# Soft-capped attention with an MLP: half-tile scores issued ahead of VectorE's reads of the same PSUM tile, and two tanh in the other order

## The chip, the cores and the metric

The kernel runs on one core of a Trainium2 chip. The metric is the device time of one execution in microseconds (us); for the kernel before it is the median of three runs. The profile is of one further execution.

## The reference

```python
scale = 1.0 / np.sqrt(q.shape[-1])                      # q, k, v: 4 x 12 x 448 x 64
scores = scale * np.matmul(q, k.transpose(0, 1, 3, 2))
scores = cap * np.tanh(scores / cap)                    # cap = 30
scores = scores - np.max(scores, axis=-1, keepdims=True)
attn = np.exp(scores)
attn = attn / (np.sum(attn, axis=-1, keepdims=True) + 1e-09)
x = np.matmul(attn, v)                                  # heads side by side: 1792 x 768
h = np.maximum(x @ w_in, 0.0)                           # w_in 768 x 2048
out = h * h @ w_out                                     # w_out 2048 x 768
```

Inputs are float32, the weights float64, which the kernel splits on the chip into two float32r words (`hi` and `lo`) each. A product of two split operands is three matmuls: hi by hi, hi by lo, lo by hi.

## The kernel before

Attention goes over 24 pairs of heads (`NP`), one pair in each turn of a loop over `n`; the two heads of a pair share the 128 partitions, 64 rows each. The 448 keys of a pair are handled in seven blocks of 64. Scores come transposed (keys in the partitions, queries along the row) in four tiles: tiles 1, 2 and 3 hold one block of keys of both heads, a "half" tile 0 the last block of both.

The score tiles lie in PSUM, in the pool `ps_s` of two buffers, each of shape 128 x 2 x 512: two halves of one PSUM bank each. In a turn they are handed out in the order tile 1, tile 2, `half`, tile 3, so that tile 1 and `half` use one buffer and tile 2 and tile 3 the other. Of the buffer of the half tile, `half[:, 0]` takes the half tile's own scores, and `half[:, 1]` takes the transposes of the next pair's q (line 347). The next pair's k is transposed into a tile of its own (`ps_t`, line 341). `take` reads the two transposed operands back on VectorE, two instructions each: a rounded copy `kqh` (line 356) and the rest `kql` (line 357); these are the operands of the next pair's scores (line 366).

ScalarE takes tanh of each score tile out of PSUM (line 373, scale 1/cap) and then exp in SBUF (line 378, scale cap). One turn behind, `sums` (line 386) adds up the probabilities with matrices of ones and `pv` (line 396) multiplies them by v. VectorE brings both to SBUF (lines 406 and 401); the sums go through DRAM (lines 408 to 425: gathered, inverted, broadcast to a tile `rb`), and `normalise` multiplies and splits the result (lines 430 to 434) a further two turns behind.

Beside that, VectorE and ScalarE decode weights of the first MLP layer in small steps (`decode`), and from n = 9 on a turn holds one `part`: six matmuls of the first layer (line 292) for a batch whose attention is done. After the loop come the rest of the first layer and the second layer (lines 661 to 663).

The attention loop runs under a manual schedule: on every engine the instructions stand in the order in which the Python code issues them. Waits between engines are put in by the framework, from the order in which the code issues accesses of the same tile. Loads of q go through SyncE's queue, those of k and v through GpSimd's.

Of the kernel before, what the change touches and what calls it, by code (L numbers as in the profile page):

```python
# [169 lines left out]
def tile_softcap_attention_mlp(ctx, tc, q, k, v, cap, w_in, w_out, out):  # L170
# [143 lines left out]
    def load_k(n, queues=(nc.sync, nc.sync)):  # L314
        for _ in load_keys(kn[n % NKQ], k, n, queues):
            pass

    def load_q(n, upper=(nc.sync, nc.sync), lower=None):
        b, j = divmod(n, NPAIR)
        for i in range(2):  # L320
            x = q[b, 2 * j + i].rearrange("(p t) d -> p t d", t=NS)
            upper[i].dma_start(out=qn[n % NKQ][top, 0:4, i], in_=x[:, 0:4])
            (lower or upper)[i].dma_start(out=qn[n % NKQ][bottom, 0:3, i], in_=x[:, 4:7])

    def load_v(n):
        for _ in load_keys(vn[n % NKV].rearrange("p h t d -> p t h d"), v, n, (nc.gpsimd, nc.gpsimd)):
            pass
# [9 lines left out]
    def transpose_k(n):  # L337
        tps[n, 0] = ps_t.tile([P, 512], F32, tag="t", name="tp")
        kf = kn[n % NKQ].rearrange("p t h d -> p t (h d)")
        for t in range(4):  # L340
            nc.tensor.transpose(tps[n, 0][:, t * P:(t + 1) * P], kf[:, t], ident)  # L341

    def transpose_q(n, tp):
        tps[n, 1] = tp
        qf = qn[n % NKQ].rearrange("p t h d -> p t (h d)")
        for t in range(3):
            nc.tensor.transpose(tp[:, t * P:(t + 1) * P], qf[:, t], ident)  # L347
        nc.tensor.transpose(tp[:, 3 * P:S], qf[top, 3], ident[top, top])

    def take(n, i, cast=nc.vector.tensor_copy):  # L350
        cols = (slice(0, 4 * P), slice(4 * P, 4 * P + S))[i]
        if i == 0:
            kqs[n] = [qp.tile([P, 4 * P + S], F32R, tag=x, name=x) for x in LATE]
        hi, lo = kqs[n]
        tp = tps.pop((n, i))[:, :cols.stop - cols.start]
        cast(out=hi[:, cols], in_=tp)  # L356
        nc.vector.tensor_sub(out=lo[:, cols], in0=tp, in1=hi[:, cols].bitcast(F32))  # L357

    def scores(n, u, sc=None):
        hi, lo = kqs[n]  # L360
        if sc is None:
            sc = ps_s.tile([P, 2, 512], F32, tag="s", name="sc")
        rows, t = ((top, bottom), u - 1) if u else ((slice(0, P),), 3)
        for s, (kx, qx) in enumerate(((hi, hi), (hi, lo), (lo, hi))):
            for h, r in enumerate(rows):
                nc.tensor.matmul(out=sc[:, h, :S], lhsT=kx[r, t * P:(t + 1) * P], rhs=qx[r, 4 * P:],  # L366
                                 start=(s == 0), stop=(s == 2))
        probs[n, u] = sc

    def tanh(n, u):  # L370
        c = 2 if u else 1
        p = pp.tile([P, c, S], F32, tag=f"p{c}", name="p", bufs=NPT if u else 2)
        nc.scalar.activation(out=p, in_=probs[n, u][:, :c, :S], func=ACTF.Tanh, scale=qks)  # L373
        probs[n, u] = p

    def exp(n, u):
        p = probs[n, u]
        nc.scalar.activation(out=p, in_=p, func=ACTF.Exp, scale=cap_sb)  # L378


    def sums(n):
        pvs[n, 1] = ps_v.tile([P, S], F32, tag="pb", name="pb")
        for u in (1, 2, 3, 0):
            for h in range(2):
                r = 32 * (h if u % 2 else 2 + h)
                nc.tensor.matmul(out=pvs[n, 1][r:r + 32], lhsT=ones if u else hones[:, h],  # L386
                                 rhs=probs[n, u][:, h if u else 0], start=(u in (1, 2)), stop=(u in (3, 0)),
                                 tile_position=(0, r))


    def pv(n):
        pvs[n, 0] = ps_v.tile([P, S], F32, tag="pa", name="pa")
        for u in range(NU):
            p, t = probs.pop((n, u)), (u - 1 if u else 3)
            for h, r in enumerate((top, bottom)):
                nc.tensor.matmul(out=pvs[n, 0][r], lhsT=vn[n % NKV][:, h, t], rhs=p[:, h if u else 0],  # L396
                                 start=(u == 0), stop=(u == NU - 1))

    def evac(n):
        es[n] = ep.tile([P, S], F32, tag="e", name="e", bufs=NE)  # L400
        nc.vector.tensor_copy(out=es[n], in_=pvs.pop((n, 0)))


    def take_sums(n):
        e = ep.tile([P, S], F32, tag="es", name="es", bufs=NE)
        nc.vector.tensor_copy(out=e, in_=pvs.pop((n, 1)))
        rds[n] = ep.tile([P - 16, 2, 8], F32, tag="cmp", name="cmp", bufs=NE)
        nc.sync.dma_start(out=rds[n][:, 0], in_=e[0:64:32])
        nc.sync.dma_start(out=rds[n][:, 1], in_=e[64:P:32])

    def invert(n):
        cmp = rds[n]
        nc.vector.scalar_tensor_tensor(out=cmp[:, 0], in0=cmp[:, 0], scalar=guard[:P - 16], in1=cmp[:, 1],
                                       op0=ALU.add, op1=ALU.add)
        nc.vector.reciprocal(out=cmp[:, 0], in_=cmp[:, 0])
        rd = dram.tile([2, S], F32, tag="rd", name="rd")
        nc.sync.dma_start(out=rd.rearrange("i (o c) -> (i o) c", c=8), in_=cmp[:, 0])
        rds[n] = rd


    def spread(n):
        rd = rds[n]
        rds[n] = ep.tile([P, S], F32, tag="rb", name="rb", bufs=2)
        for h, r in enumerate((top, bottom)):
            last["dma"] = nc.sync.dma_start(out=rds[n][r], in_=rd[h:h + 1].partition_broadcast(D))

    def normalise(n):
        b, j = divmod(n, NPAIR)
        x = ep.tile([P, S], F32, tag="x", name="x", bufs=1)
        nc.vector.tensor_mul(out=x, in0=es.pop(n), in1=rds.pop(n))  # L430
        xs = xpool.tile([P, 2, S], F32R, tag="xs", name="xs")
        hi, lo = xs[:, 0], xs[:, 1]
        nc.vector.tensor_copy(out=hi, in_=x)
        last["dve"] = nc.vector.tensor_sub(out=lo, in0=x, in1=hi.bitcast(F32))
        xh[b, j], xl[b, j] = hi, lo
# [24 lines left out]
    def prepare_cap():  # L460

        nc.vector.tensor_scalar_mul(ncap, cap_sb, -1.0)
        nc.vector.tensor_tensor(out=ncap, in0=ncap, in1=cap_sb, op=ALU.min)
        nc.vector.tensor_scalar(out=far, in0=ncap[0:1], scalar1=-CAP_MAX, scalar2=None, op0=ALU.is_lt)

        nc.scalar.activation(out=guard, in_=ncap, func=ACTF.Exp)
        nc.vector.tensor_scalar_mul(guard, guard, 1e-9)
# [24 lines left out]
    def part(pool=ps_m, tag="m"):  # L492
        b, f, o = parts.pop(0)
        if o == 0:
            hps[b, f] = pool.tile([P, 512], F32, tag=tag, name="hps")[:, :S]
        mlp1_part(b, f, o, 6)
        if o == 3 * KDM - 6:
            ends.append((b, f))

    def decode(count):  # L500
        for _ in range(count):
            next(decoding, None)


    for n in range(NP + 1):
        on, prep, old = n < NP, n + 1 < NP, n > 0
        more = n + 2 < NP

        if on:
            scores(n, 1)  # L510
            scores(n, 2)
            tanh(n, 1)
            tanh(n, 2)
            exp(n, 1)
            exp(n, 2)
        if more:
            load_q(n + 2)
            load_k(n + 2, (nc.gpsimd, nc.gpsimd))
            load_v(n + 2)
        if n == 0:  # L520
            prepare_cap()
        decode(1)

        if on:
            half = ps_s.tile([P, 2, 512], F32, tag="s", name="sc")
        if prep:
            transpose_k(n + 1)
            transpose_q(n + 1, half[:, 1])
            take(n + 1, 0)
            take(n + 1, 1)  # L530
        if on:
            scores(n, 0, half)
        if on and parts[0][1] in decoded and n >= NPAIR * (parts[0][0] + 1) + 3:
            part()
        if on:
            tanh(n, 0)
        if n >= 2:
            invert(n - 2)

        if on:  # L540
            scores(n, 3)
            tanh(n, 3)
            exp(n, 0)
            exp(n, 3)

        if n >= 3:
            normalise(n - 3)
        if old:
            sums(n - 1)
            take_sums(n - 1)  # L550
            pv(n - 1)
        if n >= 2:
            spread(n - 2)
        for b, f in ends:
            mlp1_end(b, f)
        ends.clear()
        decode(2 if n < 9 else 3)
        if old:
            evac(n - 1)
# [167 lines left out]
```

## Time and profile before

| | |
|---|---|
| time, median of three runs | 781.48 us (780.1 to 785.14) |
| profiled execution, time | 784.2 us |
| its span, first to last instruction | 782.4 us |
| TensorE busy | 721.2 us, 92% of the span |
| VectorE, ScalarE, GpSimd busy | 49%, 39%, 15% |
| mean granted TensorE clock | 0.954 of full speed |
| the attention loop | up to about 324 us |

The profile names engines PE (TensorE; PEld is its loading of weights), DVE (VectorE), ACT (ScalarE), POOL (GpSimd) and SPq (SyncE's DMA queue). L366 is line 366 of the kernel. A matmul's end is modelled, and a busy engine is not one at its peak. "A <- B" at a wait says that A stood idle until B was done.

### The profile page before, as it was taken

To read this page: it belongs to the slowest core of one execution; us is meant where nothing else is said; L and a number is where in the kernel's file an instruction comes from. 1 tells how busy PE (TensorE), PEld (TensorE's weight loads), DVE (VectorE), ACT (ScalarE), POOL (GpSimd) and SP (SyncE) were. 2 spreads that over 40 slices of the span, in tenths; PEclk is the share of its full clock that TensorE was granted. 3 is DMA by queue.
4 is the path that set the end of the run, shared out by engine and by line. 5 is a ranking of instruction groups with operands and counts; after the bars stand their busy time and mean duration, and the time that the engine had idled before them with its cause. 6 is when DMAs were issued, how large, how long until landed. Compare 5 with 4: busy or idle time off the path is not lost.

```text
span 782.4 us, 10711 instructions
## 1 busy us (share of the span) xinstructions
PE 721.2 (92%) x3978; PEld 575.5 (74%) x3978; DVE 383.3 (49%) x807; ACT 301.3 (39%) x430; POOL 114.1 (15%) x201
## 2 busy tenths in 40 slices
PE   6787787888878788999999999999999999999996
PEld 5333334445444454699899999999999999999995
DVE  3345555454554533455598999961896112111100
ACT  4657555554555554331353443421433212111100
POOL 8424424232242410010000000000000000000000
PEclk8799999898999889999999999999999999999998
DMA  7233424253243311151466456453563422342001
GB/s 169 57 80 89 109 56 104 59 112 84 67 110 81 92 51 25 49 178 65 137 217 187 134 192 192 152 168 113 172 206 95 125 75 75 93 124 79 22 21 34
DMA packets 95932, 83.11 MB, mean 106 GB/s; under 512 B 39072, under 2 KB 86688, under 8 KB 95872
## 3 DMA queue, kind: packets, MB, share of 16 engines
q1 hardware_dynamic: 86768, 68.50, 30.5%
q0 software_dynamic: 6112, 10.91, 5.9%
q10 hardware_dynamic: 2992, 2.93, 1.2%
q8 instruction: 33, 0.54, 0.3%
q14 instruction: 27, 0.22, 0.1%
HBM read 61.87 MB, written 20.27 MB: 105 GB/s over the span
## 4 chain that ended last, share of the span: by engine, by line
PE 90%; DVE 8%; ACT 1%; issue 0%
PE hps L292 31%; PE sc L366 11%; PE po L661 10%; PE po L662 10%; PE po L663 10%; PE pa L396 10%; PE pb L386 6%; DVE kql L357 4%; DVE kqh L356 4%; PE tp L341 2%; PE warm L443 1%; ACT p L373 0%; ACT p L378 0%; ACT osb L668 0%; PE tp L347 0%
## 5 line engine op out<-in xcount | busy, mean ns | idle before, releaser
L292 PE MATMUL hps<-xs,kqh 128*128 128x448 f32 x576 | 163.6, 365 | 1.3 <-DVE r L297 1.3
L661 PE MATMUL po<-ohi,gh 128*128 128x384 f32 x448 | 149.7, 335 | 0.6 <-ACT osb L668 0.6
L662 PE MATMUL po<-olo,gh 128*128 128x384 f32 x448 | 150.0, 335 | 0.0
L663 PE MATMUL po<-ohi,gl 128*128 128x384 f32 x448 | 148.4, 335 | 0.0
L373 ACT ACTIVATE p<-sc,qks 128x896 f32<-128x896 f32 (+1 forms) x96 | 85.0, 912 | 132.8 <-PE sc L366 131.5
L292 PEld LDWEIGHTS hps<-xs,kqh 128*128 128x128 f32 x576 | 108.1, 188 | 10.2 <-DVE r L297 1.7
L292 PE MATMUL hps<-xs,kql 128*128 128x448 f32 x288 | 105.2, 365 | 0.0
L366 PE MATMUL sc<-kqh 64*128 64x448 f32 (+1 forms) x168 | 47.6, 484 | 50.1 <-DVE kql L357 49.0
L614 DVE TENSOR_TENSOR gl<-graw,gh 128x2048 fp32r<-128x2048 f32 x14 | 32.1, 2291 | 124.3 <-ACT gh L613 114.0
L378 ACT ACTIVATE p<-p,cap_sb 128x896 f32<-128x896 f32 (+1 forms) x96 | 85.4, 941 | 0.0
L661 PEld LDWEIGHTS po<-ohi,gh 128*128 128x128 f32 x448 | 84.0, 188 | 0.9 <-ACT osb L668 0.9
L662 PEld LDWEIGHTS po<-olo,gh 128*128 128x128 f32 x448 | 84.1, 188 | 0.0
L663 PEld LDWEIGHTS po<-ohi,gl 128*128 128x128 f32 x448 | 84.0, 188 | 0.0
L366 PEld LDWEIGHTS sc<-kqh 64*128 64x128 f32 (+1 forms) x168 | 19.8, 202 | 80.4 <-DVE kql L357 52.2
L396 PE MATMUL pa<-p,vn 128*64 128x448 f32 x384 | 77.7, 547 | 0.0
L296 ACT ACTIVATE r<-hps 128x448 f32<-128x448 f32 x64 | 34.6, 541 | 84.0 <-PE hps L292 82.4
L396 PEld LDWEIGHTS pa<-p,vn 128*64 128x64 f32 x384 | 25.6, 138 | 54.0 <-issue 53.2
L292 PE MATMUL hps<-xs,whi 128*128 128x448 f32 x192 | 63.2, 415 | 0.0
L297 DVE TENSOR_TENSOR r<-hps,r 128x448 f32<-128x448 f32 x64 | 39.6, 620 | 48.0 <-ACT r L296 47.9
L613 ACT CAST gh<-graw 128x2048 fp32r<-128x2048 f32 x14 | 26.7, 1910 | 92.1 <-PE po L662 82.2
L292 PEld LDWEIGHTS hps<-xs,kql 128*128 128x128 f32 x288 | 54.1, 188 | 4.3
L44 ACT ACTIVATE mag<-wraw 128x384 f32<-128x384 f32 x64 | 34.9, 552 | 54.0 <-DVE olo L56 30.4
(81 smaller groups left out, 887.3 us busy)
## 6 DMA issues: line engine op xcount, KB each, us to landing
g_dram<-r SPq DMA_DIRECT2D x64, 224.0 KB
graw<-g_dram SPq DMA_DIRECT2D x14, 1024.0 KB
wraw<-in_moe_w_in_dram SPq DMA_DIRECT2D x32, 384.0 KB
wraw<-in_moe_w_out_dram SPq DMA_DIRECT2D x32, 384.0 KB
rb<-rd SPq DMA_DIRECT2D x48, 112.0 KB
vn<-in_v_dram POOLq DMA_DIRECT2D x48, 64.0 KB, 2.8
qn<-in_q_dram SPq DMA_DIRECT2D x44, 64.0 KB
kn<-in_k_dram POOLq DMA_DIRECT2D x44, 64.0 KB, 2.9
```

The costliest lines, as they stand in the source:

```text
L44: yield nc.scalar.activation(out=magf, in_=high.bitcast(F32), func=ACTF.Abs, scale=2.0 ** 16)
L292: nc.tensor.matmul(out=ps, lhsT=w[:, c * P:(c + 1) * P], rhs=x[b, c], start=(n == 0), stop=(n == 3 * KDM - 1))
L296: nc.scalar.activation(out=r, in_=ps, func=ACTF.Relu)
L297: last["square"] = nc.vector.tensor_mul(out=r, in0=ps, in1=r)
L366: nc.tensor.matmul(out=sc[:, h, :S], lhsT=kx[r, t * P:(t + 1) * P], rhs=qx[r, 4 * P:], start=(s == 0), stop=(s == 2))
L373: nc.scalar.activation(out=p, in_=probs[n, u][:, :c, :S], func=ACTF.Tanh, scale=qks)
L378: nc.scalar.activation(out=p, in_=p, func=ACTF.Exp, scale=cap_sb)
L386: nc.tensor.matmul(out=pvs[n, 1][r:r + 32], lhsT=ones if u else hones[:, h], rhs=probs[n, u][:, h if u else 0], start=(u in (1, 2)), stop= ...
L396: nc.tensor.matmul(out=pvs[n, 0][r], lhsT=vn[n % NKV][:, h, t], rhs=p[:, h if u else 0], start=(u == 0), stop=(u == NU - 1))
L661: nc.tensor.matmul(out=po[:, o, :HO], lhsT=gh, rhs=hi[:, os_], start=(f == 0), stop=False)
L662: nc.tensor.matmul(out=po[:, o, :HO], lhsT=gh, rhs=lo[:, os_], start=False, stop=False)
L663: nc.tensor.matmul(out=po[:, o, :HO], lhsT=gl, rhs=hi[:, os_], start=False, stop=(f == NF - 1))
```

## The change

The half tile's scores are issued directly after q's transposes, ahead of VectorE's four reads of the transposed operands; before, they came behind these in the code. The half tile's tanh is issued behind tile 3's tanh, and the exponentials follow in the order tile 3, half tile.

```diff
         if prep:
             transpose_k(n + 1)
             transpose_q(n + 1, half[:, 1])
+        if on:
+            scores(n, 0, half)
+        if prep:
             take(n + 1, 0)
             take(n + 1, 1)
-        if on:
-            scores(n, 0, half)
         if on and parts[0][1] in decoded and n >= NPAIR * (parts[0][0] + 1) + 3:
             part()
-        if on:
-            tanh(n, 0)
         if n >= 2:
             invert(n - 2)
 
         if on:
             scores(n, 3)
             tanh(n, 3)
+            tanh(n, 0)
+            exp(n, 3)
             exp(n, 0)
-            exp(n, 3)
```

## Rows read from the trace of the kernel before

**Rows 1.** The chain that ended last: share of the span by engine, by line.

```profile
PE 90%; DVE 8%; ACT 1%; issue 0%
PE hps L292 31%; PE sc L366 11%; PE po L661 10%; PE po L662 10%; PE po L663 10%; PE pa L396 10%; PE pb L386 6%; DVE kql L357 4%; DVE kqh L356 4%; PE tp L341 2%; PE warm L443 1%; ACT p L373 0%; ACT p L378 0%; ACT osb L668 0%; PE tp L347 0%
```

**Rows 2.** Waits, 33 to 324 us: total us, times, longest.

```profile
POOL vn L311 <- PE pa L396: 168.8, 20, 9.7
ACT p L373 <- PE sc L366: 125.4, 63, 4.7
...
PE sc L366 <- DVE kql L357: 42.9, 21, 2.0
```

**Rows 3.** Timeline of turn n = 3: start, us, instruction, [idle before <- releaser].

```profile
45.86 1.91 ACT L373 ACTIVATE p<-sc,qks 128x896 f32<-128x896 f32 x2 [3.11 <-PE sc L366]
...
47.40 0.27 PE L348 MATMUL sc<-ident,qn 64*128 64x64 f32 x1
47.65 1.97 ACT L378 ACTIVATE p<-p,cap_sb 128x896 f32<-128x896 f32 x2
...
49.03 0.62 DVE L357 TENSOR_TENSOR kql<-sc,kqh 128x448 fp32r<-128x448 f32 x1
...
49.71 0.47 PE L366 MATMUL sc<-kqh 128*128 128x448 f32 x1 [2.04 <-DVE kql L357]
...
50.52 0.47 PE L366 MATMUL sc<-kqh 64*128 64x448 f32 x2
...
50.62 0.64 ACT L373 ACTIVATE p<-sc,qks 128x448 f32<-128x448 f32 x1 [0.57 <-PE sc L366]
```

**Rows 4.** Windows, one per turn: length, engines' busy us (instructions), clock, DMA.

```profile
33.84:45.01 11.17, 9.13 (x63) 4.35 (x63) 5.61 (x11) 6.89 (x8) 4.57 (x8) 1.00 0.28 63
45.01:57.78 12.77, 10.73 (x63) 4.61 (x63) 6.27 (x13) 7.33 (x9) 4.58 (x8) 0.87 0.44 105
...
105.73:116.90 11.17, 9.13 (x63) 4.35 (x63) 7.13 (x14) 6.90 (x8) 4.58 (x8) 1.00 0.34 83
116.90:130.81 13.91, 11.87 (x70) 6.16 (x69) 6.83 (x14) 7.33 (x9) 4.58 (x8) 0.88 0.39 96
...
186.45:200.42 13.97, 11.93 (x69) 6.64 (x69) 7.38 (x15) 7.83 (x10) 4.55 (x8) 0.88 0.44 97
...
228.03:240.41 12.38, 10.34 (x69) 5.48 (x69) 7.41 (x15) 7.72 (x10) 4.58 (x8) 1.00 0.32 76
...
296.08:309.88 13.80, 11.76 (x69) 6.68 (x69) 5.65 (x11) 6.89 (x8) 0.00 (x0) 0.88 0.07 19
309.88:324.28 14.40, 13.91 (x92) 6.10 (x92) 6.99 (x15) 7.10 (x9) 0.00 (x0) 1.00 0.18 51
```

**Rows 5.** Windows of 1 us, same columns as rows 4.

```profile
48.00:49.00 1.00, 0.00 (x0) 0.00 (x0) 1.00 (x2) 1.00 (x2) 1.00 (x3) 1.00 0.80 193
...
52.00:53.00 1.00, 1.00 (x12) 0.38 (x8) 0.00 (x0) 1.00 (x3) 0.00 (x0) 0.50 0.15 26
```

**Rows 6.** Timeline of the loop's start, n = 0 and 1.

```profile
14.84 0.55 ACT L44 ACTIVATE mag<-wraw 128x384 f32<-128x384 f32 x1 [1.62 <-DMA wraw<-in_moe_w_in_dram]
...
15.96 0.74 PE L366 MATMUL sc<-kqh 128*128 128x448 f32 x1 [4.79 <-DVE kql L357]
...
18.67 0.57 PE L366 MATMUL sc<-kqh 64*128 64x448 f32 x2
...
22.36 0.55 PE L347 MATMUL sc<-ident,qn 128*128 128x128 f32 x3 [0.66 <-ACT p L373]
...
24.48 0.74 PE L366 MATMUL sc<-kqh 128*128 128x448 f32 x1 [1.37 <-DVE kql L357]
```

**Rows 7.** Window of the start, same columns as rows 4.

```profile
16.00:33.84 17.84, 15.81 (x72) 7.65 (x72) 4.61 (x9) 10.31 (x13) 6.41 (x11) 0.68 0.28 62
```

**Rows 8.** Timeline of n = 23: half scores, and the reader of the broadcast.

```profile
311.78 0.47 PE L366 MATMUL sc<-kqh 128*128 128x448 f32 x1 [0.49 <-ACT p L373]
...
312.14 0.62 DVE L430 TENSOR_TENSOR x<-e,rb 128x448 f32<-128x448 f32 x1 [1.22 <-DMA rb<-rd]
```

## The prediction

> **What bounds the kernel now.** I read the chain that ended last first: 90% of it is TensorE, 8% VectorE, and the VectorE part is two lines, 356 and 357, the reads (`take`) that follow the transposes [rows 1]. So TensorE is the pace-maker and hands the chain over to VectorE in one place only. The list of waits over the attention loop says where: the score matmuls of line 366 wait for line 357 21 times, 42.9 us in all, 2.04 us each, and that is TensorE's only wait of size there [rows 2]. GpSimd and ScalarE wait for TensorE instead (168.8 and 125.4 us), so neither sets the pace. The timeline of one turn (n = 3) shows the wait itself: the last transpose of q starts at 47.40 and is over at 47.67, VectorE's fourth read ends at 49.65, and the half tile's first matmul starts at 49.71 [rows 3]. That matmul writes `half[:, 0]` from keys and queries that were ready a turn ago; VectorE reads `half[:, 1]`. All that the two share is the tile, so the wait is one of order on a tile and not of data.
>
> The table by turns gives what the wait costs [rows 4]. One turn without MLP part (n = 2) is 11.17 us long with 9.13 us of TensorE work, the difference being the 2.04. Others, such as the next, take 12.77 us for the same instructions, and their granted clock is 0.87 instead of 1.00. With a part it is 12.38 us (10.34 of work) at clock 1.00 and mostly 13.8 to 13.9 at 0.88. In windows of a microsecond the clock falls from 1.00 to 0.50 (from 2.4 to 1.2 GHz) after the stretch in which TensorE did nothing [rows 5]. Three of the seven turns without a part and thirteen of the fourteen with one have such a stretch, and in each the engine's idle 2 us are in progress or less than 2 us past when it begins. The last turn (n = 23) has no transposes and no wait for VectorE, and it and its end run at 1.00 [rows 4].
>
> **The change part by part.** TensorE's own order stays as it was (transposes of k, of q, half scores, part, scores of tile 3), for the reads are VectorE's; VectorE's order stays too. What moves is which of the two comes first on the shared tile. ScalarE's order does change. No DMA and no queue entry moves.
>
> *The wait removed.* The half scores need the buffer's free half, which q's transposes ahead of them have already waited for. They can follow at 47.67: minus 2.04 us for each of n = 2 to 22. What is late next? Their own successor, scores of tile 3, needs the buffer that the tanh of tile 2 leaves; that tanh (the second of two in 1.91 us from 45.86) ends at 47.77 [rows 3], and half scores of 0.81 us (from 49.71 to tile 3's first at 50.52) from 47.67 end at 48.5. Nothing else in the row of TensorE work is waited for, so the turn becomes its work: 9.13 us, and 10.34 with a part.
> Over n = 2 to 8, from 33.84 to 116.90, 83.06 us become 7 x 9.13 = 63.9: 19.15 less, 14.3 of it the wait and 4.9 the slow clock. Over n = 9 to 22, from 116.90 to 309.88, 192.98 us become 14 x 10.34 = 144.8: 48.2 less, 28.5 the wait and 19.7 the slow clock [rows 4]. I take the full clock because each slow stretch follows an idle stretch that goes away; the other end is nothing of these 24.5 us.
>
> *The wait added.* VectorE's third read (the cast of q) may now wait for the half scores, as they write the same tile just before. They end at about 48.5, and the read began at 48.38, as its end at 49.65 less two reads of 0.6 shows [rows 3]. So 0.1 to 0.3 us on VectorE, and behind it stand inversion, normalisation and the reading of the sums. VectorE works at most 7.4 us of a turn [rows 4]; the reads end near 49.9 and the next turn's scores want them at 45.01 + 9.13 = 54.14. Hidden by 4 us; cost nothing.
>
> *ScalarE's order.* Tile 3's tanh goes ahead of the half tile's, and so waits for scores of tile 3. Without a part these take as long again and end at 49.3, while ScalarE is in its exponentials until 47.65 + 1.97 = 49.62, or 50.2 with a decode instruction. Then come 0.96 (half of 1.91) and 0.64 us of tanh [rows 3], and the half tile's buffer is free at 51.8. The next scores want it at 54.14: 2.3 us spare. With a part (10.34 less 9.13, 1.2 us at full clock) tile 3's scores end near 50.5, the buffer is free at 52.3 and wanted at 55.35: 3 us spare. The swap of exponentials is free, since sums read them a turn later. If that cover were gone, each microsecond by which ScalarE is late would be one on TensorE; ScalarE's work is 6.9 to 7.8 us of the 9.13 [rows 4].
>
> *The other queues at the quicker pace.* GpSimd's loads of v and k take at most 4.6 us of a turn, and it waits for TensorE with them [rows 2, 4]. The broadcast of the reciprocals is nearest to being late: in n = 23, the one turn without the wait of 2 us, VectorE waited 1.22 us for it, until 312.14 [rows 8]. In the changed kernel this use comes about 5 us after the turn's start, behind four reads of VectorE's, where in n = 23 it comes 2.3 us after it (at 309.88) with none before it. I take nothing; bounds are 0 and that row's 1.22 us on VectorE, which has 1.7 us or more idle in a turn.
>
> *The start.* In n = 0 the half scores wait 4.79 us, from 11.17 to 15.96, and in n = 1 another 1.37 [rows 6]. VectorE's reads for n = 1 end at 15.9 either way, and its scores need the half tile's buffer too: ScalarE's decode instruction ends at 15.39, and the tanh of tile 3 and of the half behind it at 17.0. They can begin there, and began at 18.67: 1.6 us are sure. ScalarE's exponentials (0.98 for the wide one, half of 1.97, and some 0.64 for the half, as its tanh) then end at 18.6 and the next tile's tanh at 19.6; q's transposes, which wait for that tanh, go then and not at 22.36, and the half scores behind their 0.75 us (24.48 less 1.37 less 22.36) at 20.4 and not at 24.48: 4.1 us. Bounds are 1.6 and 6.2 (both waits whole); I take 4.7, nearer the second, as this stretch runs at a mean clock of 0.68 [rows 7] and gains a little more when its idle time shrinks.
>
> *The sum.* 19.15 + 48.2 + 4.7 = 72 us. All after the loop (from 324.28) is the same work at clock 1.00 and stays. The span of 782.4 becomes 710.3, the profiled time of 784.2 becomes 712. The median of the runs is 781.5, 2.7 lower, so between 709.5 and 712: I say 711.
>
> **The rivals.** *The wait goes, the clock does not come back.* What slows it would be not the idle 2 us but the pattern of matmuls. For it: five turns have the same idle stretch and no slow one. Against it: no slow stretch begins without an idle one just before, and n = 23 runs full. Price: 14.3 + 28.5 + 4.7 = 47.5, so 736.7 in the profiled execution, some 735 as median. The Trainium skill ("TensorE: Matmul & The Clock Gate", section "A second HAM failure mode: psum-queue depth-cycling") tells of a kernel in which short idles between groups of matmuls, as it went through PSUM banks, kept the clock going between its levels without long gaps. By that rule a kernel that turns over its score buffers this often might keep oscillating, and 735 would be the time; the trace so far speaks against it, as the last row of rows 4 has the same groups at 1.00.
>
> *The wait moves.* TensorE reaches a place where something else is late: the half buffer's tanh, or the broadcast. If the 2.04 us and the slow clock stay in another place, the time is that of now, 781; if half of both does, 784 - 36 = 748. For it: n = 23, without the other wait, has a new one of 0.49 us for ScalarE [rows 8]; against it: that is the tanh of tile 1, which the transposes cover in all other turns, and the spare times above.
>
> *The change does not do what it says*: the half scores still stand behind VectorE for another reason (a shared buffer of keys). Then ScalarE's reorder alone is left, 781. Against it: in n = 23, where there is nothing to read, they do not wait for VectorE.
>
> *Slower.* The one mechanism is the half buffer held longer on ScalarE: its release now stands behind tile 3's tanh, which stands behind the part. Up to 3.0 us of lateness it costs nothing; it eats the whole gain of a turn with a part (13.8 less 10.34, 3.4 us) at 6.4 us of lateness, and at 7 it is 14 x 0.6 = 8 us slower, 790. ScalarE would need to stand idle for most of a turn in front of tile 3's tanh; nothing of that length is in its row.
>
> **How the numbers follow.** Wait and clock both gone: 0.72, with 703 (the start at its bound, all else whole) to 722 (half a microsecond left in each of 21 turns). Clock stays, wholly or for the larger part: 0.15, 722 to 738. The wait moves: 0.07, half of it at 745 to 770 and half near 781. Not what it says: 0.03, 781. Slower: 0.03. The range of 703 to 738 leaves out 0.13. One per cent, 8 us, is about what a measurement can tell here. Faster by more: 0.72 + 0.15 + 0.04 = 0.91; within it: 0.03 + 0.03 = 0.06; slower: 0.03.
>
> **What would show it.** In the changed profile: TensorE's waits for line 357 gone from the list; turns of 9.1 and 10.3 us; clock near 1.00 from about 30 us on; the part's six matmuls in 1.2 us everywhere; the chain nearly all TensorE; the third read a little later. Wrong would be: a new wait of TensorE on line 373 (the half buffer), a clock of 0.9 in turns without an idle stretch, or VectorE waiting for the broadcast and TensorE for VectorE.

## The result, and the profile after

The changed kernel takes 709.4 us (median of four runs, 707.6 to 711.2), the kernel before 783.3 us (four runs): a ratio of 0.906, 95% interval 0.902 to 0.910. The forecast was 711.

The profiled execution took 711.2 us with a span of 709.4, 73.0 less than the 782.4 of before. Its page begins as follows: span, busy time and share of each engine, and further down the chain that ended last.

```profile
span 709.4 us, 10732 instructions
...
PE 694.6 (98%) x3978; PEld 559.8 (79%) x3978; DVE 385.0 (54%) x807; ACT 297.9 (42%) x430; POOL 114.4 (16%) x201
...
PE 97%; DMA 1%; ACT 1%; SPq 0%; DVE 0%; issue 0%
```

TensorE is busy 98% of the span, and the 8% of the chain that ran over VectorE's two lines [rows 1] are 0%. TensorE's work itself fell from 721 to 695 us with the same 3978 matmuls, which is mostly the slow clock that went (26.0 us of it in the loop; a stretch of the first layer, below, took 3.3 us more). The list of TensorE's waits over the loop after its start (26.66 to 248.26 us) has one line left where [rows 2] had 42.9 us:

```profile
PE sc L366 <- ACT p L373: 0.5, 1, 0.5
```

That is the wait of n = 23 that was there before [rows 8]. The windows by turns (columns as in rows 4) answer to [rows 4]: n = 2, n = 8, two turns with a part, and the last.

```profile
26.66:35.73 9.07, 9.07 (x63) 4.37 (x63) 5.71 (x11) 6.67 (x8) 4.58 (x8) 1.00 0.34 78
...
81.06:90.12 9.06, 9.06 (x63) 4.36 (x63) 7.14 (x14) 6.68 (x8) 4.58 (x8) 1.00 0.42 103
90.12:100.39 10.27, 10.27 (x70) 5.49 (x69) 6.92 (x14) 7.22 (x9) 4.58 (x8) 1.00 0.52 131
...
182.53:192.79 10.26, 10.26 (x69) 5.48 (x69) 7.67 (x16) 7.22 (x9) 4.58 (x8) 1.00 0.58 154
...
233.86:248.26 14.40, 13.91 (x92) 6.10 (x92) 7.00 (x15) 7.22 (x9) 0.00 (x0) 1.00 0.18 51
```

Length and TensorE's work are now the same number in each turn, and the clock is 1.00 in all of them. The timeline of one turn without a part (n = 6) shows what [rows 3] showed before:

```profile
65.31 0.27 PE L348 MATMUL sc<-ident,qn 64*128 64x64 f32 x1
...
65.51 0.47 PE L366 MATMUL sc<-kqh 128*128 128x448 f32 x1
...
65.69 0.69 DVE L357 TENSOR_TENSOR kql<-tp,kqh 128x512 fp32r<-128x512 f32 x1
...
66.42 0.62 DVE L356 CAST kqh<-sc 128x448 fp32r<-128x448 f32 x1
...
67.08 0.62 DVE L357 TENSOR_TENSOR kql<-sc,kqh 128x448 fp32r<-128x448 f32 x1
...
67.90 1.52 ACT L373 ACTIVATE p<-sc,qks 128x896 f32<-128x896 f32 x2
...
71.92 0.47 PE L366 MATMUL sc<-kqh 64*128 64x448 f32 x2
```

The half scores start 0.2 us after the last transpose's start instead of 2.3 us, while VectorE is in its first two reads. VectorE's third read starts 0.73 us after the second's start (66.42 against 65.69); in turn n = 3 of before it was 0.60 us, as these rows show:

```profile
47.78 0.69 DVE L357 TENSOR_TENSOR kql<-tp,kqh 128x512 fp32r<-128x512 f32 x1
...
48.38 0.61 DVE L356 CAST kqh<-sc 128x448 fp32r<-128x448 f32 x1
```

So the wait for the half scores, whose last matmul ends at about 66.4, costs VectorE 0.13 us in a turn, and TensorE nothing. The two tanh end at 69.42, and the next turn's scores start at 71.92.

**Where the 73.0 us came from.** The start (up to the first scores of n = 2) is 33.84 - 26.66 = 7.2 us shorter. The loop from there to its end took 290.44 us and takes 221.60: 68.8. After the loop 3.0 us are lost again: 458.1 became 461.1. These are in the stretch of the first MLP layer, the long run of line 292, whose first row below is of the kernel before and the second of the changed one:

```profile
372.68:540.75 168.07, 168.07 (x829) 155.77 (x830) 132.53 (x313) 62.50 (x122) 1.02 (x1) 1.00 0.53 166
```

```profile
296.80:468.18 171.38, 171.38 (x829) 155.70 (x830) 133.03 (x313) 62.19 (x122) 1.01 (x1) 1.00 0.50 163
```

Instructions, busy time of the other engines and clock are the same. The last experiment comes back to it.

### The profile page after: what moved, and what is told of

It is laid out like the page before. It is cut to its first block, busy times and chain, and to the rows that moved or that the text cites. A ratio compares the mean times of both kernels' runs of the same rounds, so it can differ in the third digit from the quotient of the medians.

```text
span 709.4 us, 10732 instructions
## 1 busy us (share of the span) xinstructions
PE 694.6 (98%) x3978; PEld 559.8 (79%) x3978; DVE 385.0 (54%) x807; ACT 297.9 (42%) x430; POOL 114.4 (16%) x201
## 4 chain that ended last, share of the span: by engine, by line
PE 97%; DMA 1%; ACT 1%; SPq 0%; DVE 0%; issue 0%
PE hps L292 33%; PE po L661 11%; PE po L662 11%; PE po L663 11%; PE pa L396 11%; PE sc L366 10%; PE pb L386 6%; PE tp L341 2%; PE sc L347 1%; DMA wraw<-in_moe_w_in_dram 1%; PE sc L348 1%; PE warm L443 1%; ACT p L373 0%; SPq L323 0%; SPq L322 0%; ACT osb L668 0%
## 5 line engine op out<-in xcount | busy, mean ns | idle before, releaser
L292 PE MATMUL hps<-xs,kqh 128*128 128x448 f32 x576 | 165.5, 368 | 1.3 <-DVE r L297 1.3
L373 ACT ACTIVATE p<-sc,qks 128x896 f32<-128x896 f32 x96 | 82.5, 911 | 60.5 <-PE sc L366 60.5
L378 ACT ACTIVATE p<-p,cap_sb 128x896 f32<-128x896 f32 x96 | 85.7, 946 | 0.0
L292 PE MATMUL hps<-xs,whi 128*128 128x448 f32 x192 | 54.0, 362 | 0.0
L366 PE MATMUL sc<-kqh 64*128 64x448 f32 (+1 forms) x168 | 43.3, 445 | 4.8 <-ACT p L373 4.2
L668 ACT COPY osb<-po 128x384 f32<-128x384 f32 x28 | 13.2, 477 | 70.3 <-PE po L663 60.0
```

The costliest lines, as they stand in the source:

```text
L292: nc.tensor.matmul(out=ps, lhsT=w[:, c * P:(c + 1) * P], rhs=x[b, c], start=(n == 0), stop=(n == 3 * KDM - 1))
```

## The experiments

My theory: TensorE waited for the order of accesses on one tile and for nothing else; the slow clock came from the idle time that this wait made; ScalarE's order is worth nothing. The rivals: ScalarE's order carries a share; the clock falls by the pattern of the matmuls, whatever the idle time; the half scores wait for data.

**One part at a time.** Half scores moved, ScalarE's order as before (against the changed kernel):

```diff
+        if on:
+            tanh(n, 0)
         if n >= 2:
             invert(n - 2)
...
             tanh(n, 3)
-            tanh(n, 0)
-            exp(n, 3)
             exp(n, 0)
+            exp(n, 3)
```

> Half scores ahead of VectorE's reads, ScalarE's order as before (half tile's tanh first, its exponential first). Theory, that the wait on the shared tile was everything: ScalarE has over 2 us to spare in a turn, so its order is worth nothing and the time is that of the whole change, 709 us, within 4. Rival, that the later tanh carries a share (a half buffer or tile 3's exponential that comes free in better time): 716 or more, and TensorE waits for line 373 in the loop.

Measured: 710.0 us (709.0 to 711.9), ratio 0.908 (0.904 to 0.911). The turns have the same 9.07 and 10.27 us as in the changed kernel, and the list of TensorE's waits in the loop is the same single line as after. The moved scores alone make the whole gain.

ScalarE's order alone (against the changed kernel, the reads ahead of the half scores again):

```diff
-        if on:
-            scores(n, 0, half)
         if prep:
             take(n + 1, 0)
             take(n + 1, 1)
+        if on:
+            scores(n, 0, half)
```

> Only ScalarE's order is changed, the half scores still stand behind the four reads. Theory: the wait of 2.04 us and the slow clock both stay, 783 us within 4. Rival as in the run beside it: some of the 74 us, so 776 or less.

Measured: 784.7 us, ratio 1.002 (1.000 to 1.005) over ten runs. TensorE's list of waits, over the whole span:

```profile
PE sc L366 <- DVE kql L357: 49.6, 24, 4.8
PE sc L366 <- ACT p L373: 1.6, 2, 1.1
```

The wait is as it was (in this execution the slow clock came in seventeen of the twenty-one turns, in that of before in sixteen), and the second part of the change moves nothing that can be measured, up or down.

**Order or data.** Everything in the order of the kernel before, but q's transposes in another tile:

```diff
-            transpose_q(n + 1, half[:, 1])
+            transpose_q(n + 1, ps_v.tile([P, S], F32, tag="pb", name="tq"))
```

> Order of the kernel before on all engines, but q's transposes go into the PSUM tile of the sums, free at that time, instead of the half tile's buffer. Theory, that the half scores waited for a read of the same tile and for no data: they go at once, as in the changed kernel; the sums must then wait for the reads, which costs some 0.6 us in each of the seven turns without a part and nothing where a part lies between: 709 + 4 = 713, within 4. Rival, that they wait for VectorE for another reason (operands, a buffer of keys): 783.

Measured: 712.0 us, ratio 0.910 (0.907 to 0.913). TensorE's waits, over the whole span:

```profile
PE pb L386 <- DVE cmp L413: 4.5, 7, 0.7
PE sc L366 <- ACT p L373: 3.3, 2, 2.8
...
PE sc L366 <- DVE kql L357: 0.2, 1, 0.2
```

With the half tile's buffer left to the half tile, the same half scores, issued behind the reads in the code as before, no longer wait for them. The sums now do, 0.64 us in each of the seven turns without a part (4.5 in all, where I had worked out 4). The releaser is given as line 413, which stands right behind the reads on VectorE. So the wait was for the tile. No turn here runs slowly (9.66 to 9.68 us without a part), though TensorE stands idle 0.64 us in seven of them. In the fourteen turns with a part this kernel is even quicker, 10.14 us against 10.27: its eight transposes take 1.12 us (189.26 to 190.38) and not 1.24.

**Idle time or pattern.** The kernel before with TensorE's wait filled:

```diff
             transpose_q(n + 1, half[:, 1])
+            fill = ps_v.tile([P, S], F32, tag="pb", name="fill")
+            for _ in range(NFILL):                      # NFILL = 8
+                nc.tensor.matmul(out=fill[:, :P], lhsT=zero, rhs=zero, start=True, stop=True)
             take(n + 1, 0)
```

> The kernel before, with eight matmuls of zeros (128 columns each) put into TensorE's wait; their result is not used. They write the tile that the sums use later, so they wait for nothing. Theory, that the idle stretch is what brings the clock down: the wait stays about 2 us, the clock rises to 1.00 in the loop, and 24.5 us of 783 go, some more at the start: 755 to 760. Rival, that the pattern of matmuls brings it down: clock still 0.87 to 0.88 in most turns and 783, or a little more if the eight outlast the wait.

Measured: 757.2 us (756.9 to 757.6), ratio 0.968 (0.964 to 0.971). The timeline of one turn, and the window of that turn:

```profile
186.14 2.05 PE L532 MATMUL fill<-zero 128*128 128x128 f32 x16
188.26 0.47 PE L366 MATMUL sc<-kqh 128*128 128x448 f32 x1
```

```profile
183.49:195.87 12.38, 12.32 (x87) 7.35 (x85) 7.13 (x14) 7.34 (x9) 4.58 (x8) 1.00 0.37 95
```

The trace counts two instructions for each of the eight float32 matmuls, as it does for the sums. The half scores start as late as ever, 2.1 us after the transposes, but every turn runs at full clock: 11.18 to 11.19 us without a part, 12.38 to 12.41 with one, the lengths that only five turns of twenty-one had before. The twenty-one turns take 251.7 us where they took 276.0. So 24 us of the 74 are the clock's in the loop, and they come back when work of no use fills the idle time, with the other matmuls and their buffers as they were. The Trainium skill ("TensorE: Matmul & The Clock Gate", section "A second HAM failure mode: psum-queue depth-cycling") tells of a kernel cycling through PSUM banks in which short idles between groups of matmuls make the clock go between its levels. In this case the turning over of the buffers alone does not do it: this kernel and the changed one turn them over in the same way at clock 1.00, and what they lack is the idle stretch.

**How much idle time.** The changed kernel with the half scores behind some of the reads again; the four reads are functions of their own here, a cast and a rest for k and for q:

```diff
-        if on:
-            scores(n, 0, half)
         if prep:
             take(n + 1, 0)
-            take(n + 1, 1)
+            cast_q(n + 1)
+        if on:
+            scores(n, 0, half)
+        if prep:
+            rest_q(n + 1)
```

> The changed kernel with a part of the wait put back: the half scores stand behind the two reads of k and the cast of q, and only the last read (0.62 us, 0.65 with its gap) comes after them. TensorE is idle 1.4 us in each of 21 turns. If the clock stays up: 709 + 21 x 1.4 = 738. If an idle stretch of this length brings it down as often as that of 2.04 us did: up to 24 more, 762. Theory: in between, a smaller number of slow turns than the sixteen of before.

Measured: 750.6 us (748.0 to 754.0), ratio 0.959 (0.956 to 0.963). And with the half scores earlier by one read:

```diff
-        if on:
-            scores(n, 0, half)
         if prep:
-            take(n + 1, 0)
-            take(n + 1, 1)
+            cast_k(n + 1)
+            cast_q(n + 1)
+        if on:
+            scores(n, 0, half)
+        if prep:
+            rest_k(n + 1)
+            rest_q(n + 1)
```

> As the run beside it, with the half scores behind the two casts only (k, then q), and both rests after them: TensorE is idle about 0.7 us in each of 21 turns. Clock up: 709 + 21 x 0.7 = 724. Theory: no slow stretch in the loop, 724 within 4. Rival, that any regular idle stretch keeps the clock going between its levels: slow turns as before, 740 or more.

Measured: 730.9 us, ratio 0.933 (0.930 to 0.935), outside the 724 within 4. TensorE's waits in the loop of the first kernel, and of the second (line 381 is the score matmul, 361 the cast of q):

```profile
PE sc L381 <- DVE kqh L361: 29.0, 21, 1.4
```

```profile
PE sc L381 <- DVE kqh L361: 15.0, 21, 0.7
```

And the clock, for the first kernel in its three slow stretches and the loop, for the second in its loop (columns: length, TensorE's work, clock, DMA):

```profile
58.00:62.00 4.00, 4.00 (x24) 0.60 0.13 30
123.50:127.50 4.00, 4.00 (x19) 0.57 0.23 60
195.00:199.00 4.00, 4.00 (x13) 0.57 0.47 94
32.00:285.80 253.80, 224.27 (x1442) 0.98 0.36 90
```

```profile
30.00:265.20 235.20, 219.67 (x1444) 1.00 0.40 97
```

Idle 2.04 us, sixteen slow turns of twenty-one; idle 1.4 us, three; idle 0.7 us, none. So it isn't any regular idle time that brings the clock down. Each count is of one profiled execution; that of the first kernel here was the quickest of its four, and the others, up to 6.0 us longer, may have had more slow turns.

Not all that the first kernel takes beyond 738 is the slow clock. The span of its profiled execution is 36.8 us above that of the changed kernel: 30.6 us by 1.45 us more in each of 21 turns (10.52 us without a part, 11.73 with one), 4.7 us by the three slow turns, and 5.3 us by the start, where the half scores of n = 0 wait 3.11 us for the cast; 3.9 us go the other way after the loop, most of them in the stretch of line 292.

My 724 for the second kernel failed by 7 us, and not in the clock. Its turns are 0.79 to 0.80 us longer than those of the changed kernel where I had put 0.7 (9.86 and 11.07 against 9.07 and 10.27), which makes 16.7 us instead of 14.7. The start adds 3.4 us: TensorE waits 3.41 us there for the cast, runs slowly after it, and the first product with v starts at 26.82 and not at 23.43. I had left the start out. The remaining 1.5 us are in what was compared: both profiled executions have the longer stretch of line 292, while the 709 from which I counted is a median that lies 1.9 us below the changed kernel's profiled execution.

**ScalarE's spare time.**

```diff
             tanh(n, 3)
-            tanh(n, 0)
             exp(n, 3)
+            tanh(n, 0)
             exp(n, 0)
```

> The changed kernel with the half tile's tanh one step later still, behind tile 3's exponential: the half buffer comes free 1.0 us later. By the spare times of the prediction (2.3 us without a part, 3.0 with) it costs nothing: 709 within 4, TensorE without a new wait. If the spare times were wrong by more than 1.3 us, up to 1 us in each turn: 715 to 731.

Measured: 708.8 us (708.1 to 709.0), ratio 0.905 (0.902 to 0.907): the same as the changed kernel. TensorE's waits in its loop are the one line of 0.5 us again. A buffer that comes free 1.0 us later costs nothing, as it should with 2.5 us in hand without a part (turn n = 6, above) and some 3.1 with one.

**Two attempts at more.**

```diff
+        if n == 0:
+            prepare_cap()
...
-        if n == 0:
-            prepare_cap()
-        decode(1)
+        if n:
+            decode(1)
...
-            tanh(n, 3)
-            tanh(n, 0)
+            for u in (3, 0) if n else (0, 3):
+                tanh(n, u)
+            if n == 0:
+                decode(1)
```

> The changed kernel with the start in another order: the small instructions on the cap go ahead of the loop, the first decode step behind the tanh of turn 0, and in turn 0 the half tile's tanh ahead of tile 3's. In the changed kernel TensorE waits 3.7 us for ScalarE there, until 16.1 us. Theory: VectorE's reads no longer stand behind the exponential that it waits for, the scores of n = 1 begin near 14.5, and 1.5 to 2.5 us go: 707. Rival, that loads of q and k for the next turns are then late: no change, 709.

Measured: 708.5 us, no different from 709.4. TensorE's waits (whole span) and its timeline at the start say why:

```profile
PE tp L341 <- DMA kn<-in_k_dram: 2.5, 2, 2.3
PE sc L366 <- ACT p L373: 1.8, 2, 1.3
```

```profile
13.82 0.47 PE L366 MATMUL sc<-kqh 64*128 64x448 f32 x2 [1.29 <-ACT p L373]
...
17.89 1.09 PE L341 MATMUL tp<-ident,kn 128*128 128x128 f32 x4 [2.29 <-DMA kn<-in_k_dram]
```

The scores of n = 1 begin 2.3 us earlier (13.82 against 16.10), and then TensorE waits 2.29 us for the load of k. That was the rival.

```diff
+            behind = on and parts[0][1] in decoded and n >= NPAIR * (parts[0][0] + 1) + 3
-            transpose_q(n + 1, half[:, 1])
+            transpose_q(n + 1, ps_v.tile([P, S], F32, tag="pb", name="tq") if behind else half[:, 1])
```

> The changed kernel, with q's transposes in the sums' tile in the fourteen turns that have a part, and in the half tile's buffer in the others. With that tile such a turn took 10.14 us instead of 10.27, and the sums' wait of 0.6 us arose only in turns without a part. Expected: 14 x 0.13 = 1.8 us less than the run beside it. Rival: a wait of the sums for the reads appears in turns with a part as well, no change or a few us more.

> The changed kernel once more, as the measure for the run beside it, and for one open point: in its first profile the long stretch of the first MLP layer took 171.4 us, 3.3 more than in the kernel before and in six of the eight profiles of other kernels, with the same instructions at granted clock 1.00. If the change causes it, it is there again, 171.4; if it comes and goes by itself, 168.1 is as likely. Time 709 within 3.

Measured on one chip, six runs each: 706.4 us with the tile by turn, 709.2 for the changed kernel again; their ratios to the kernel before, 0.901 (0.897 to 0.904) and 0.903 (0.900 to 0.907), overlap, so the medians alone don't settle it. The turns with a part take 10.14 us as expected, 14 x 0.13 = 1.8 us less in the loop. The lists of runs show the open point: the changed kernel has three at 707.3 to 707.8 and three at 710.6 to 711.0, the other five at 705.8 to 706.9 and one at 709.4. A step of some 3.2 us comes and goes between executions of one program. In the profiles a step of that size is in the stretch of line 292, which here was 171.38 us for the changed kernel again (a run of its upper group) and 168.08 for the other (a run of its lower group). That the two steps are the same follows from their size; no program was profiled in both groups. Against equals (707.6 and 706.2, the medians of the quicker groups) the new tile is worth about 1.4 us, near its 1.8, and this is the quickest kernel of the study, by a margin that the intervals can't confirm.

## Why the prediction was right

- **The wait on the tile** (42.9 us in 21 turns): gone, and nothing of it came back elsewhere in the loop. That it was order on a tile and not data was an inference from two rows; the other tile for q shows it.
- **The slow clock** (24.5 us, taken whole, with nothing as the other end): whole. The filled wait separates it from the wait: 24.3 us in the same turns with the wait still there. The rival in which the clock stays is refuted by that run.
- **The turns**: worked out as 9.13 and 10.34 us, measured 9.07 and 10.27. The difference is in where the half scores can start: worked out was the end of q's last transpose (47.40 and 0.27 us, so 47.67), but they start 0.20 us after its start (65.51 after 65.31), as the trace lets a matmul begin before the one ahead of it has ended. So the wait was worth 2.11 us in a turn and not 2.04. Over 21 turns the 0.07 us are the 1.5 us by which the loop gained more (68.84 against 67.35).
- **The added wait** on VectorE: 0.1 to 0.3 us worked out, 0.13 in the turn shown, and hidden, as priced.
- **ScalarE's order**: 2.3 us spare worked out without a part, 2.5 seen (69.42 to 71.92); 3.0 with one, 3.1 seen in the turn from 182.5 us on. The order alone measured 1.002, and a step later still costs nothing. The rival on the slow side had nothing to start from.
- **The broadcast**: taken as nothing. VectorE waits for it twice in the loop, 2.4 us in all (2.6 before), and no wait of TensorE follows from it.
- **The start** is the term that was mis-sized: 4.7 us taken, 6.2 as its bound, 7.2 measured. The steps went about as worked out (scores of n = 1 at 16.10 instead of 18.67, worked out 17.0; q's transposes at 19.50 instead of 22.36, worked out 19.6; half scores at 20.18 instead of 24.48, worked out 20.4). The step that failed was the bound, which took both waits whole and left the clock out of it: of the 7.2 us, 4.3 were gained by the half scores of n = 1 (24.48 less 20.18), and the other 2.9 behind them, where TensorE has no idle time in either kernel but took 9.29 us at clock 0.66 and takes 6.41 at 1.00. The window from 16 us to the first scores of n = 2 ran at 0.84 where [rows 7] had 0.68:

```profile
16.00:26.66 10.66, 10.56 (x63) 5.69 (x63) 4.28 (x8) 9.14 (x13) 6.51 (x12) 0.84 0.48 102
```

The size is of this execution. Three profiles have this start in the code: the changed kernel again gains 7.3 us in it, the kernel with the tile by turn 6.0, where ScalarE's decode instruction waits for its load until 15.80 and not 14.61. So the bound was passed in two of three.

- **All after the loop stays**: 3.0 us off in the profiled execution, by the stretch of line 292. The times of the changed kernel show a step of the same size between runs of one program, so it is no fixed price of the change. Both profiles of the changed kernel had the long form, as had one of the ten other kernels'; whether the change makes it more frequent is not shown.

So 72 us worked out and 73.0 measured stand close together partly because two errors, the start's 2.5 us and the loop's 1.5, met one of 3.0 in the other direction.

## What to carry to other kernels

When an engine waits in every turn for a reader of a tile and not for its data, look at what else shares that tile: issuing the writer first, or giving one of the two another tile, removes the wait. Here the first was worth 74 us and the second 70, as the other tile brought a wait of 4.5 us with it. Price such a wait with the clock it costs: of 74 us, a third was TensorE running at 1.2 GHz for a few microseconds after sixteen of the twenty-one idle stretches. And before counting on a reorder on an engine that is not the bound, work out its spare time: here 2.5 us or more in a turn, so that its order could be changed either way at no cost or gain.

## What the runs showed of the hardware that was not expected

- The clock fell after idle stretches of 2.04 us in sixteen of twenty-one turns, after 1.4 us in three, after 0.7 us in none (one profiled execution each; another kernel with the stretch of 2.04 us had seventeen). Eight matmuls of zeros in the idle stretch kept it at 1.00, though the waiting work started as late as before.
- The stretch of 829 matmuls of line 292 took 168.07 to 168.09 us or 171.38 us, at granted clock 1.00 both times: 202.7 or 206.7 ns from one to the next. Of twelve profiles of kernels whose code there is the same, nine had the first value and three the second (the changed kernel twice); runs of one program differ by about the same 3.2 us. What chooses between them stays open.
- q's and k's transposes took 1.12 us with q's in the sums' tile and 1.24 with q's in the score buffer, for the same eight instructions. The cause was not followed up.
